# Attention and two expert layers on one core: VectorE's order in the front left to the scheduler, weight conversion cut into pieces, late weight splits spread out

## The chip, the cores and the metric

The kernel runs on one core of a Trainium2 chip. The metric is device time in microseconds for one execution, from the median of several runs. Five engines take part, each with its own in-order queue: TensorE (PE, with its weight loads PEld), VectorE (DVE), ScalarE (ACT), GpSimd (POOL) and SyncE (SP, which here issues nearly all DMAs).

## What is computed

The reference, cut to what matters here:

```python
scores = q @ k.T / 8 + bias; attn = softmax(scores in a causal window of 128)    # 4 x 8 heads, 576 x 64
x = attn @ v                                          # 2304 tokens x 512
h = x @ w_in; g = maximum(0.01 * h, h); x = g @ w_out # d_ff 2048
logits = x @ w_gate                                   # 8 experts
# tokens go to experts by descending logit, at most 288 tokens to an expert
for e in range(8): out[mask_e] = maximum(x[mask_e] @ w1[e], 0) @ w2[e]
```

w_in and w_out arrive as 64-bit floats; the kernel turns them into 32-bit ones on the chip. All large products are made with operands split into a high and a low part (three products each), so every weight needs a copy on ACT (high) and a subtraction on DVE (low).

## The kernel before

There are three stages. The **front** (0 to about 418 us) does attention, the first product (x @ w_in) and the logits; the middle (to about 660 us) does the second product and, beside it, the assignment of tokens; the end runs the eight experts. The change touches the front alone.

The front is a loop over steps s. A step handles one block of 64 queries at several stages of its life: scores of block s+1 on PE, its four score reductions on DVE (L435, `neg` and `nm`) and four exponentials on ACT (L438, `pr`), the weighted sum of block s-1 (L479, `xv`), the transposes of block s (L462, `pt`, copied by ACT as `pts`, L464) and the normalisation of block s+1: DVE makes the reciprocal (L446, L447, `rs`) and ACT multiplies by it (L450; from block 13 on DVE takes half, L452). In every second step ACT copies a finished pair of blocks (L489, `xh`) and DVE subtracts (L490, `xl`). Beside this a step runs up to four **items** before step 16, two from then on: an item is 24 matmuls of x @ w_in into one bank `h` (L504; there are two such banks), ACT's scaled copy `th` (L513) and DVE's maximum into `gb` (L517), which sets the bank free. Items stand in fixed steps: two in 5 and 8, four in 9, 11, 13, 14 and 15, two in each from 17 on.

Sixteen weight tiles are converted, k = 0 to 15, in steps `CONV_AT` = 2, 3, 5, 6, 8, 9, 10, 11, 13, 14, 16, 17, 19, 20, 22, 23. ACT takes the absolute value one step ahead (`conv_abs`, L343). DVE does two operations in `conv_first` (L354, L355) and four in `conv_rest` (L361, L364, L365, L367), all in place on `dt` with a helper `de`. For k < 8 ACT then writes the high part (L348, `wh_in`) as the last thing in the step, and DVE the low part one step later (L371, `wl_in`). For k of 8 and more the result is w_out, written to memory and folded with w_gate on PE (`wtp`, `pg`, `pw`, and `gs` on DVE).

What sets the order: PE, ACT and DVE run in the order in which the program is written (`ENG_A`, `manual_schedule`). So `conv_rest` stands as one block of four behind the first item's `gb`, and `conv_first` behind `xl`. SP and POOL are left to the scheduler.

From step 28 on the loop also loads and splits late tiles (`tail`: three of w_out, two of g, five of w_out) through two staging tiles (L167 `st_out`, L157 `wh_out`, L158 `wl_out`): twice per step it splits the oldest staged tile and stages the next, the first three at once, the others when few items are left. Late logits use bank t, the bank of the transposes; it is set free by a small copy on DVE (L544, `lt`).

Of the kernel before, what the change touches and what calls it, by code (L numbers as in the profile page):

```python
# [33 lines left out]
PTB = 2  # L34
PRB = 2
ET = mybir.EngineType
ENG_A = {ET.PE, ET.Activation, ET.DVE}
F_GE = {32: 6, 64: 9}
F_NB = 3
F_TOT = 6  # L40
# [84 lines left out]
def tile_attn_moe_moe2(ctx: ExitStack, tc: tile.TileContext, q_in, k_in, v, w_in, w_out, w_gate, w1, w2, consts, out):  # L125
    nc = tc.nc
    V, A, T, GP = nc.vector, nc.scalar, nc.tensor, nc.gpsimd
# [28 lines left out]
    def split_weight(st, wh, wl, lo_engine):  # L156
        A.activation(wh, st, AF.Copy)  # L157
        lo_engine.tensor_tensor(out=wl, in0=st, in1=wh.bitcast(F32), op=ALU.subtract)  # L158
# [5 lines left out]
    def stage(src, name, pool=None, after=None):  # L164
        pool = pool or stp
        st = pool.tile([P, 1024], F32, tag="wst", name=f"st_{name}", bufs=2 if pool is stp else 3)
        d = nc.sync.dma_start(st, src)  # L167
        if after is not None:
            tc.add_manual_dep(d.ins, after.ins.name, SYNC, reason="behind the first gather")
        return st  # L170
# [128 lines left out]
    by_hand = ctx.enter_context(ExitStack())  # L299
    by_hand.enter_context(tc.manual_schedule(engines=ENG_A))  # L300
    with ExitStack() as actx:
# [39 lines left out]
        def conv_abs(k):  # L341
            t = cv.tile([P, 1024], F32, tag="dt", name=f"dt_{k}", bufs=DTB)
            A.activation(t, raws[k][:, :, 1].bitcast(F32), AF.Abs)  # L343
            conv[k] = t
# [12 lines left out]
        def conv_rest(k):  # L357

            t = conv[k]
            ti = t.bitcast(I32)  # L360
            V.scalar_tensor_tensor(out=ti, in0=raws[k][:, :, 1], scalar=-0x40000000, in1=ti,  # L361
                                   op0=ALU.bitwise_and, op1=ALU.bitwise_or)
            e = cv.tile([P, 1024], F32, tag="de", name=f"de_{k}", bufs=1)
            V.tensor_single_scalar(e.bitcast(I32), ti, -0x800000, op=ALU.bitwise_and)  # L364
            V.scalar_tensor_tensor(out=e, in0=raws.pop(k)[:, :, 0].bitcast(U32), scalar=2.0 ** -52,  # L365
                                   in1=e, op0=ALU.mult, op1=ALU.mult)
            V.tensor_tensor(out=t, in0=t, in1=e, op=ALU.add)  # L367

        def in_low(k):
            wh, wl = win[k]  # L370
            V.tensor_tensor(out=wl, in0=conv.pop(k), in1=wh.bitcast(F32), op=ALU.subtract)  # L371
# [190 lines left out]
        items = [(c, fp) for c in range(NCH) for fp in range(8)]  # L562
# [19 lines left out]
        if True:  # L582
# [19 lines left out]
            def prepare(j):  # L602

                if j and j % 3 == 0:
                    load_qk(j // 3 + 1)

            ready, in_ready = {}, {}
            s = 0
            pending, low_next = [], []
            tail = [(None, wout, wo_dram[fp], f"out_{fp}") for fp in range(3)]  # L610
# [3 lines left out]
            staged = []  # L614
# [4 lines left out]
            while s <= max(NQ, late_end) or items or pending or tail:  # L619

                now = [x for x in items if max(ready.get(x[0], 1 << 30), in_ready.get(x[1] | 1, 1 << 30)) <= s]
                now = now[:ITEMS_0 if s < ITEMS_S else 2]
                for x in now:
                    items.remove(x)
                k = conv_at.get(s)

                for f in after.pop(s, ()):
                    f[0](*f[1:])
                if s + 1 < NQ:
                    scores(s + 1)  # L630
                    prepare(s + 1)
                for k2 in transposes_of_gate:
                    gate_transpose(k2)
                transposes_of_gate.clear()
                if s + 1 < NQ:
                    softmax_exp(s + 1)
                if 0 < s <= NQ:
                    weighted(s - 1)
                    if (s - 1) % 4 == 3:
                        ready[(s - 1) // 4] = s + XLAG  # L640
                for k2 in products_of_gate:
                    gate_product(k2)
                products_of_gate.clear()
                if s < NQ:
                    transpose_p(s)
                load_v(s + 2)
                if k is not None:
                    conv_first(k)
                if s + 1 < NQ:
                    softmax_norm(s + 1)  # L650
                for k2 in low_next:
                    in_low(k2)
                low_next.clear()
                done, pending = pending, []
                if done and not items and not now:
                    fill(F_A)
                for f in done:
                    f[0](*f[1:])
                for c in loads_late:
                    late_load(c)  # L660
                loads_late.clear()
                if s + 1 in conv_at:
                    conv_abs(conv_at[s + 1])
                for n, (c, fp) in enumerate(now):
                    expand(c, fp, 0)
                    expand(c, fp, 1)
                    expand_out(c, fp)
                    if fp % 2 == 1 and c >= LG0:
                        pending.append((logits, c, fp // 2, gbs[c], "l"))
                        if fp == 7:  # L670
                            at(s + 2, logits_fold, c)
                    if n == 0 and k is not None:
                        conv_rest(k)
                if k is not None:
                    if not now:
                        conv_rest(k)
                    if k < 8:
                        in_high(k)
                        low_next.append(k)
                        in_ready[k] = s + IN_LAG  # L680
                    load_raw(k + RAWB)
                if s == gate_end:
                    cv.release()
                    wpa = ctx.enter_context(tc.tile_pool(name="wpa", bufs=3, side="right"))
                    stp = ctx.enter_context(tc.tile_pool(name="stp", bufs=2, side="right"))
                    late_pool = tc.alloc_tile_pool(name="late", bufs=1, side="right")
                if s == late_end:
                    late_pool.release()
                for _ in range(2):
                    if s > gate_end and tail:  # L690
                        if staged and (len(tail) > 7 or len(items) <= len(tail)):
                            pool, lst, _, name = tail.pop(0)
                            lst.append(weight_tiles(pool or wpa, name))
                            split_weight(staged.pop(0), *lst[-1], V)
                        for _, _, src, name in tail[len(staged):STAGES]:
                            staged.append(stage(src, name))
                s += 1
            fill(F_A2)
            for f in sorted(after):
# [409 lines left out]
```

## Time and profile before

| what | value |
|---|---|
| time, median of 3 runs | 920.09 us (920.0 to 920.4) |
| the profiled execution, its own time | 918.32 us |
| its span, first to last instruction | 916.2 us |
| PE busy | 848.8 us (93%) |
| DVE busy | 526.6 us (57%) |
| ACT busy | 392.8 us (43%) |
| mean granted TensorE clock | 0.96 |

A share of busy time is a mean over stages with different limits. The front has to be read by itself: in its first 180 us PE is busy for four to nine tenths of a slice and its granted clock is below 1, later it is busy nearly all the time. Which engine ends each wait there is read from the waits, the chain that ended last and the timeline.

### The profile page before, as it was taken

The page shows a single profiled execution, that of the slowest core. Times are in us where ns is not written, and L with a number is a line of the kernel's source. Part 1 is how long each engine was busy: PE and PEld are TensorE (multiplying, and loading weights), DVE is VectorE, ACT ScalarE, POOL GpSimd, SP SyncE. Part 2 cuts the span into 40 slices and gives each one's busy share as a digit, 9 for nine tenths or more (in the row PEclk, how much of TensorE's full clock was granted, in tenths as well). Part 3 has the DMA queues.
Part 4 walks back from the last instruction along what each step waited for, and adds up shares of the span by engine and source line. Part 5 has one row for each costly group of instructions (what it writes and reads, how often), then busy time and mean ns, then how long its engine had stood idle before and what let it go on. Part 6 is the DMA issues. An engine that isn't in the chain of part 4 may idle for free.

```text
span 916.2 us, 18584 instructions
## 1 busy us (share of the span) xinstructions
PE 848.8 (93%) x7590; PEld 738.8 (81%) x7590; DVE 526.6 (57%) x1311; ACT 392.8 (43%) x867; POOL 56.0 (6%) x82
## 2 busy tenths in 40 slices
PE   5668878989999899999999999998999999999996
PEld 3557767878889788887677777776889999999995
DVE  3866766376674534247678777676235554555540
ACT  6756453456664544232212121211225555555551
POOL 1000000000000000000000000000020221122211
PEclk9578899989999999999999999998999999999998
DMA  9863644577455996585423324221426655576630
GB/s 292 252 199 107 190 145 136 175 212 218 134 164 145 290 238 171 144 249 145 143 93 107 115 80 131 87 95 55 138 91 190 189 182 170 192 223 203 189 119 26
DMA packets 103636, 147.18 MB, mean 161 GB/s; under 512 B 6144, under 2 KB 74368, under 8 KB 101504
## 3 DMA queue, kind: packets, MB, share of 16 engines
q1 hardware_dynamic: 100480, 136.56, 49.7%
q0 software_dynamic: 3072, 9.44, 3.0%
q8 instruction: 60, 0.98, 0.4%
q14 instruction: 24, 0.20, 0.1%
HBM read 113.21 MB, written 32.77 MB: 159 GB/s over the span
## 4 chain that ended last, share of the span: by engine, by line
PE 68%; DVE 14%; ACT 10%; issue 4%; DMA 1%; POOL 1%; SPq 0%; ACTq 0%; POOLq 0%; DVEq 0%
PE po L221 22%; PE h L504 13%; PE m L987 10%; PE y L1006 10%; ACT pr L438 4%; PE cnt L807 3%; PE lg L531 2%; DVE de L365 2%; DVE gb L517 2%; ACT pr L450 2%; DVE dt L361 2%; PE xv L479 2%; DVE dt L367 2%; PE pt L462 1%; ACT dt L343 1%
## 5 line engine op out<-in xcount | busy, mean ns | idle before, releaser
L221 PE MATMUL po<-wh_out,gol 128*128 128x512 f32 x272 | 112.5, 413 | 4.7 <-DVE gol L189 4.6
L517 DVE TENSOR_TENSOR gb<-h,th 128x512 f32<-128x512 f32 x72 | 49.2, 690 | 112.2 <-ACT th L513 112.2
L504 PE MATMUL h<-xh,wh_in 128*128 128x256 f32 x576 | 98.1, 294 | 14.4 <-DVE gb L517 14.3
L221 PE MATMUL po<-wh_out,goh 128*128 128x512 f32 x272 | 110.9, 408 | 0.0
L221 PE MATMUL po<-wl_out,goh 128*128 128x512 f32 x272 | 110.6, 407 | 0.0
L504 PEld LDWEIGHTS h<-xh,wh_in 128*128 128x128 f32 x576 | 80.5, 197 | 21.8 <-DVE gb L517 16.8
L504 PE MATMUL h<-xh,wl_in 128*128 128x256 f32 x576 | 92.3, 284 | 0.0
L504 PE MATMUL h<-xl,wh_in 128*128 128x256 f32 x576 | 91.3, 282 | 0.0
L181 ACT ACTIVATE goh<-gin 128x1024 fp32r<-128x1024 f32 x34 | 36.0, 1059 | 127.4 <-DMA gin<-g_dram 127.1
L158 DVE TENSOR_TENSOR wl_w<-st_w,wh_w 128x1024 fp32r<-128x1024 f32 x60 | 72.9, 1225 | 24.6 <-ACT wh_w L157 24.1
L513 ACT ACTIVATE th<-h 128x512 f32<-128x512 f32 x72 | 42.0, 593 | 104.0 <-PE h L504 103.9
L504 PEld LDWEIGHTS h<-xh,wl_in 128*128 128x128 f32 x576 | 79.8, 195 | 0.0
L438 ACT ACTIVATE pr<-neg,nm 128x192 f32<-128x192 f32 (+2 forms) x144 | 61.0, 425 | 43.4 <-DVE nm L435 43.2
L504 PEld LDWEIGHTS h<-xl,wh_in 128*128 128x128 f32 x576 | 78.6, 193 | 0.0
L1006 PE MATMUL y<-hh,wh_w 128*128 128x288 f32 x256 | 77.4, 302 | 0.0
L1006 PE MATMUL y<-hh,wl_w 128*128 128x288 f32 x256 | 75.6, 295 | 0.0
L1006 PE MATMUL y<-hl,wh_w 128*128 128x288 f32 x256 | 75.5, 295 | 0.0
L221 PEld LDWEIGHTS po<-wh_out,gol 128*128 128x128 f32 x272 | 51.7, 190 | 16.0 <-DVE gol L189 6.3
L157 ACT ACTIVATE wh_w<-st_w 128x1024 fp32r<-128x1024 f32 x60 | 62.4, 1053 | 0.9 <-DMA st_w<-in_w_dram 0.8
L221 PEld LDWEIGHTS po<-wl_out,goh 128*128 128x128 f32 x272 | 51.7, 190 | 10.3 <-issue 0.2
L221 PEld LDWEIGHTS po<-wh_out,goh 128*128 128x128 f32 x272 | 51.7, 190 | 9.5
L990 DVE SCALAR_TENSOR_TENSOR hl<-m,hh 128x288 fp32r<-128x288 f32 x64 | 29.1, 455 | 51.8 <-ACT hh L989 49.1
(219 smaller groups left out, 1545.6 us busy)
## 6 DMA issues: line engine op xcount, KB each, us to landing
st_w<-in_w_dram SPq DMA_DIRECT2D x64, 512.0 KB, 4.1
g_dram<-gb SPq DMA_DIRECT2D x72, 256.0 KB, 4.3
gin<-g_dram SPq DMA_DIRECT2D x34, 512.0 KB, 3.9
gr<-g_dram SPq DMA_DIRECT2D x48, 256.0 KB, 6.0
v<-in_v_dram SPq DMA_DIRECT2D x28, 384.0 KB, 5.5
raw<-in_w_in_dram SPq DMA_DIRECT2D x8, 1024.0 KB, 7.2
raw<-in_w_out_dram SPq DMA_DIRECT2D x8, 1024.0 KB, 5.5
x_dram<-xo SPq DMA_DIRECT2D x17, 256.0 KB, 2.2
```

What stands on the lines that cost most here:

```text
L157: A.activation(wh, st, AF.Copy)
L158: lo_engine.tensor_tensor(out=wl, in0=st, in1=wh.bitcast(F32), op=ALU.subtract)
L181: A.activation(wh, st, AF.Copy)
L221: T.matmul(po, g, w, start=(k == 0), stop=(k == 47))
L438: A.activation(pr[:, i, :nk], neg[:, a, :nk], AF.Exp, scale=-1.0, bias=nm[:, i:i + 1], accum_out=sm[:, i:i + 1])
L504: T.matmul(hp[:, j, :], w[:, d, j * P:(j + 1) * P], x[:, d, :], start=(k == 0), stop=(k == 11))
L513: A.activation(th, hp, AF.Copy, scale=0.01)
L517: V.tensor_tensor(out=gbs[c][:, o:o + 2, :], in0=hp, in1=th, op=ALU.max)
L807: T.matmul(cnt, ge[:, i, :], oh[:, i, :], start=(i == 0), stop=(i == NB - 1))
L987: T.matmul(hp, w[:, d, :], x[:, d, :], start=(k == 0), stop=(k == 11))
L990: V.scalar_tensor_tensor(out=hl[:, f, :], in0=hp, scalar=0.0, in1=hh[:, f, :].bitcast(F32), op0=ALU.max, op1=ALU.subtract)
L1006: T.matmul(yp, w, x[:, f, :], start=(k == 0), stop=(k == 23))
```

## The change

DVE leaves `ENG_A`: in the front the scheduler now chooses DVE's order, by its own estimate of when each instruction can start; PE and ACT still run as written. `conv_rest` becomes a generator, cut into its four operations, and the step calls it a piece at a time between items (one piece per item with more than two items, two with fewer, the remainder at the end). The first three late tiles are split only when they were staged two or more steps ago, one per step; the other seven keep their rule.

```diff
-ENG_A = {ET.PE, ET.Activation, ET.DVE}
+ENG_A = {ET.PE, ET.Activation}
...
             V.scalar_tensor_tensor(out=ti, in0=raws[k][:, :, 1], scalar=-0x40000000, in1=ti,
                                    op0=ALU.bitwise_and, op1=ALU.bitwise_or)
+            yield
             e = cv.tile([P, 1024], F32, tag="de", name=f"de_{k}", bufs=1)
             V.tensor_single_scalar(e.bitcast(I32), ti, -0x800000, op=ALU.bitwise_and)
+            yield
             V.scalar_tensor_tensor(out=e, in0=raws.pop(k)[:, :, 0].bitcast(U32), scalar=2.0 ** -52,
                                    in1=e, op0=ALU.mult, op1=ALU.mult)
+            yield
             V.tensor_tensor(out=t, in0=t, in1=e, op=ALU.add)
...
+                rest = iter(()) if k is None else conv_rest(k)
                 for n, (c, fp) in enumerate(now):
...
-                    if n == 0 and k is not None:
-                        conv_rest(k)
+                    for _ in range(1 if len(now) > 2 else 2):
+                        next(rest, None)
+                for _ in rest:
+                    pass
                 if k is not None:
-                    if not now:
-                        conv_rest(k)
...
-                for _ in range(2):
+                for _ in range(2 if len(tail) <= 7 else 1):
                     if s > gate_end and tail:
-                        if staged and (len(tail) > 7 or len(items) <= len(tail)):
+
+                        if staged and (staged[0][1] < s - 1 if len(tail) > 7 else len(items) <= len(tail)):
                             pool, lst, _, name = tail.pop(0)
                             lst.append(weight_tiles(pool or wpa, name))
-                            split_weight(staged.pop(0), *lst[-1], V)
+                            split_weight(staged.pop(0)[0], *lst[-1], V)
                         for _, _, src, name in tail[len(staged):STAGES]:
-                            staged.append(stage(src, name))
+                            staged.append((stage(src, name), s))
```

PE's order and POOL's do not move at all, and ACT's only in the three late `wh_out`. The number of instructions is the same but for one DMA. In the changed file lines 364 and on stand one to three lines lower up to L450, and three lower in the rest of the loop (L365, L367, L370 there are L364, L365, L367 here; L449 and L450 are L446 and L447, L520 is L517, L547 is L544).

DVE in step 5 (two items, h_0 and h_1; tile k = 2 is dt_457, tile 3 is dt_527), before:

```order
L446 TENSOR_SCALAR rs_520<-sm_473 128x4
L447 RECIPROCAL rs_520<-rs_520 128x4
L517 TENSOR_TENSOR gb_0_556<-h_0_529,th_0_554 128x512
L361 SCALAR_TENSOR_TENSOR dt_457<-raw_107,dt_457 128x1024
L364 TENSOR_SCALAR de_559<-dt_457 128x1024
L365 SCALAR_TENSOR_TENSOR de_559<-raw_107,de_559 128x1024
L367 TENSOR_TENSOR dt_457<-dt_457,de_559 128x1024
L517 TENSOR_TENSOR gb_0_556<-h_1_563,th_1_588 128x512
```

The same place now:

```order
L361 SCALAR_TENSOR_TENSOR dt_457<-raw_107,dt_457 128x1024
L449 TENSOR_SCALAR rs_520<-sm_473 128x4
L365 TENSOR_SCALAR de_559<-dt_457 128x1024
L450 RECIPROCAL rs_520<-rs_520 128x4
L367 SCALAR_TENSOR_TENSOR de_559<-raw_107,de_559 128x1024
L370 TENSOR_TENSOR dt_457<-dt_457,de_559 128x1024
L354 TENSOR_SCALAR dt_527<-dt_527 128x1024
L520 TENSOR_TENSOR gb_0_556<-h_0_529,th_0_554 128x512
L355 TENSOR_SCALAR dt_527<-dt_527 128x1024
L361 SCALAR_TENSOR_TENSOR dt_527<-raw_314,dt_527 128x1024
L520 TENSOR_TENSOR gb_0_556<-h_1_561,th_1_586 128x512
L365 TENSOR_SCALAR de_668<-dt_527 128x1024
```

Tile 2 is now finished ahead of the first item's maximum, tile 3 is begun a step early between the two maxima, and the reciprocal stands behind two pieces.

DVE in step 9 (four items; tile k = 5 is dt_811, tile 6 is dt_944), before:

```order
L446 TENSOR_SCALAR rs_936<-sm_893 128x4
L447 RECIPROCAL rs_936<-rs_936 128x4
L371 TENSOR_TENSOR wl_in_878<-dt_741,wh_in_877 128x1024
L517 TENSOR_TENSOR gb_0_973<-h_0_946,th_0_971 128x512
L361 SCALAR_TENSOR_TENSOR dt_811<-raw_596,dt_811 128x1024
L364 TENSOR_SCALAR de_976<-dt_811 128x1024
L365 SCALAR_TENSOR_TENSOR de_976<-raw_596,de_976 128x1024
L367 TENSOR_TENSOR dt_811<-dt_811,de_976 128x1024
L517 TENSOR_TENSOR gb_0_973<-h_1_980,th_1_1005 128x512
L517 TENSOR_TENSOR gb_2_1037<-h_2_1010,th_2_1035 128x512
L517 TENSOR_TENSOR gb_2_1037<-h_3_1039,th_3_1064 128x512
```

The same place now:

```order
L449 TENSOR_SCALAR rs_936<-sm_893 128x4
L370 TENSOR_TENSOR dt_811<-dt_811,de_1006 128x1024
L450 RECIPROCAL rs_936<-rs_936 128x4
L354 TENSOR_SCALAR dt_944<-dt_944 128x1024
L520 TENSOR_TENSOR gb_0_973<-h_0_946,th_0_971 128x512
L355 TENSOR_SCALAR dt_944<-dt_944 128x1024
L520 TENSOR_TENSOR gb_0_973<-h_1_976,th_1_1001 128x512
L361 SCALAR_TENSOR_TENSOR dt_944<-raw_675,dt_944 128x1024
L365 TENSOR_SCALAR de_1134<-dt_944 128x1024
L367 SCALAR_TENSOR_TENSOR de_1134<-raw_675,de_1134 128x1024
L520 TENSOR_TENSOR gb_2_1035<-h_2_1008,th_2_1033 128x512
L370 TENSOR_TENSOR dt_944<-dt_944,de_1134 128x1024
```

All six operations on tile 6 have moved out of step 10 in among the maxima of step 9, with one operation at most between the first two maxima.

DVE at the end of step 29, where the late splits stood, before:

```order
L452 TENSOR_SCALAR pr_3841<-pr_3841,rs_3877 128x192 x2
L517 TENSOR_TENSOR gb_0_3911<-h_0_3884,th_0_3909 128x512
L517 TENSOR_TENSOR gb_0_3911<-h_1_3913,th_1_3938 128x512
L158 TENSOR_TENSOR wl_out_3944<-st_out_3800,wh_out_3943 128x1024
L158 TENSOR_TENSOR wl_out_3950<-st_out_3806,wh_out_3949 128x1024
L544 COPY lt<-pl_3955 128x16
L435 ISA neg_0_3972,nm_3969<-s_0_3959,bias_sb 128x192
```

The same place now:

```order
L455 TENSOR_SCALAR pr_3835<-pr_3835,rs_3871 128x192 x2
L520 TENSOR_TENSOR gb_0_3905<-h_0_3878,th_0_3903 128x512
L547 COPY lt<-pl_3937 128x16
L520 TENSOR_TENSOR gb_0_3905<-h_1_3907,th_1_3932 128x512
L438 ISA neg_0_3954,nm_3951<-s_0_3941,bias_sb 128x192
```

Both splits have left the step (the three now stand one each in steps 30 to 32), and the copy that sets bank t free is ahead of the second maximum.

## Rows read from the trace of the kernel before

**Rows 1.** Busy time by stretch: PE, PEld, DVE, ACT, POOL, clock, DMA share, GB/s.

```profile
core 0: us, PE busy (x) PEld busy (x) DVE busy (x) ACT busy (x) POOL busy (x), PEclk, DMA share, GB/s
18.00:166.00 148.00, 111.76 (x1150) 100.71 (x1151) 101.04 (x230) 84.19 (x225) 0.29 (x1) 0.84 0.60 179
166.00:193.00 27.00, 23.62 (x294) 21.48 (x293) 13.00 (x37) 13.72 (x37) 0.00 (x0) 0.89 0.58 164
193.00:312.00 119.00, 117.81 (x1419) 108.73 (x1419) 75.58 (x222) 71.40 (x211) 0.00 (x0) 1.00 0.64 186
312.00:330.00 18.00, 14.90 (x167) 11.98 (x165) 7.64 (x20) 7.91 (x18) 0.00 (x0) 0.81 0.96 243
```

**Rows 2.** Waits: who waited for whom, total us, times, longest us.

```profile
ACT wh_in L348 <- DVE dt L367: 18.8, 6, 4.2
...
ACT pr L450 <- DVE rs L447: 15.4, 12, 1.9
...
PE h L504 <- DVE gb L517: 14.3, 11, 3.3
```

**Rows 3.** Chain that ended last, steps 5 and 6: start, us, what.

```profile
43.00 1.02 ACT dt L343
...
49.14 0.49 ACT th L513
49.65 0.69 DVE gb L517
50.34 1.14 DVE dt L361
51.51 0.71 DVE de L364
52.24 1.24 DVE de L365
53.50 1.24 DVE dt L367
54.76 1.06 ACT wh_in L348
...
58.08 0.69 DVE xl L490
58.77 0.61 DVE dt L354
...
60.39 1.11 DVE wl_in L371
...
65.92 1.06 ACT wh_in L348
```

**Rows 4.** The same chain: a reduction, and the exponentials that begin step 12.

```profile
128.02 0.26 DVE neg L435
128.32 1.86 ACT pr L438 x8
```

**Rows 5.** Timeline of steps 10 and 11: idle time before and its releaser in brackets.

```profile
105.23 1.50 ACT L450 ACTIVATE pr<-pr,rs 128x192 f32<-128x192 f32 x4 [1.90 <-DVE rs L447]
...
110.66 1.06 ACT L348 ACTIVATE wh_in<-dt 128x1024 fp32r<-128x1024 f32 x1 [2.90 <-DVE dt L367]
...
117.07 0.74 PE L504 MATMUL h<-xh,wh_in 128*128 128x256 f32 x4 [3.30 <-DVE gb L517]
```

**Rows 6.** Timeline of PE in step 16.

```profile
186.16 0.63 PE L402 MATMUL pw<-cst,gs 128*128 128x32 f32 x4 [2.64 <-DVE gs L395]
```

**Rows 7.** Timeline of PE in step 30.

```profile
318.18 1.06 PE L462 MATMUL pt<-cst,pr 128*96 128x128 f32 x4 [3.10 <-DVE lt L544]
```

**Rows 8.** The chain: two items in steps 30 and 31.

```profile
320.25 7.37 PE h L504 x48
...
332.95 5.67 PE h L504 x48
```

## The prediction, made before the changed kernel ran

> **What bounds the kernel now.** I read the busy time by stretch first [rows 1], then the waits [rows 2], then the chain that ended last [rows 3, 4]. The stretches show three regimes in the front. From 18 to 166 us (steps 2 to 14) no engine is full: PE 111.8 of 148 us at a granted clock of 0.84, DVE 101.0, ACT 84.2. From 193 to 312 us (steps 17 to 29) PE is busy for 117.8 of 119 us at clock 1.00, so it is the bound, and DVE and ACT have a third to spare. From 312 to 330 us PE is held up again, at clock 0.81.
>
> Why nobody is full early shows in the waits: ACT waits 18.8 us, in six waits, for a converted tile before it can write the high part, 15.4 us for reciprocals, and PE 14.3 us in eleven waits for a maximum that would free its bank [rows 2]. The chain shows how these hang together in step 5 [rows 3]: the first item's `th` at 49.14, its maximum at 49.65, and only then L361, L364, L365, L367 one behind another until 54.73, then `wh_in` at 54.76. DVE runs the four pieces behind a maximum that has to wait for PE and ACT, though their tile was ready at 44.02 (the end of L343). ACT cannot go on, since `wh_in` stands ahead of the next step's exponentials in its queue. So it is a ring: ACT waits for the conversion, the conversion for an item, the item for PE, PE for the last step's ACT. PE's and ACT's orders stay, so only DVE's part of this ring can become shorter. Every step keeps its items; a step that ends earlier lets all later ones start earlier, up to the middle stage, where PE is again the bound.
>
> **The change, part by part.** I walk the new DVE order with the durations of the chain. *Steps 5 and 6.* The absolute value ends at 44.02. L354 takes 0.61, and L355 I count as L364, 0.71; then L361 1.14, reciprocal and sum 0.3, L364 0.71, L365 1.24, L367 1.24: tile 2 is done near 50.0 instead of 54.73. `wh_in` now waits for the second item's `th`, which ends near 52.2, so it begins about 2.5 us sooner. What is late next is the exponentials: DVE has put L354, L355 and L361 of tile 3 and the two maxima (0.69 each) ahead of the reductions, so they start only near 54.9, 0.9 sooner than at the end of `wh_in` before (55.82). But tile 3 is then three parts done. After the low part (1.11), four reductions (0.26 each [rows 4]), `xl` 0.69, L365 and L367 it ends near 61.1; the reciprocal follows, ACT normalises, and `wh_in` starts near 62.8 instead of 65.92: 3.1 us for the two steps.
>
> *The other steps by the same walk.* Steps 2 to 4: the conversions no longer wait behind `xl` and the reductions are done while ACT still writes `wh_in`: 1.4 us. Steps 8 and 9: about 1.9 gained in step 8 as in step 5, 0.9 lost in step 9, where the reciprocal is put behind a low part and two pieces, so that the absolute value and the first `th` come later: 1.0 us. Step 10 has no item, and its tile was converted in step 9 while DVE waited for `th`: ACT's two waits there, 1.90 and 2.90 [rows 5], go: 4.8 us. Step 11: the four pieces leave the gap between the first two maxima, so the 3.30 us that PE waited [rows 5] go; the reciprocal behind two pieces costs 0.9: 2.4 us. I thus put the exponentials that began at 128.32 [rows 4] near 115.6, a sum of 12.7.
>
> Steps 13 and 14: of the 14.3 us that PE waits for maxima I count 4.4 there; tile 8's L367 and tile 9's L354 now stand ahead of step 13's first maximum and make PE wait some 2.4: 2.0 us. Step 16 has no item, and PE is idle for 3.4 of the 27 us around it [rows 1]: `gs` stood behind `xl` and made PE wait 2.64 us [rows 6]; now it is the first thing after the reductions: 2.5 us. Steps 17 to 28: PE is full [rows 1], so I take nothing. One piece between maxima is covered by 5.67 us of item work per step [rows 8]; without that cover each would cost its 0.7 to 1.2 us.
>
> *Late splits.* In step 29 two splits stand ahead of `lt`, the copy that frees the transposes' bank, and the second waited for its load. PE waits 3.10 us [rows 7], and the two items behind it take 7.37 us instead of 5.67 at the lower clock [rows 1, 8]: 3.1 + 1.7 = 4.8 us. Now the loads are two steps old and one split per step (1.1 us on DVE, as L371 in rows 3) lies beside 5.67 us of items.
>
> *What it adds.* The reductions now run bank by bank, so ACT's second exponential waits for the third reduction: 3 x 0.26 = 0.78 us after the start, against 0.26 + 1.86/4 = 0.73 when ACT gets to it. An estimate of 0.1 us a step; where a piece stands between them too, 0.7. The walk has it. On SP the loads of raw tiles are ahead of some loads of v and stores of g. A raw load waits for L365 of the tile three before, which now comes sooner, and DMA is busy for 0.60 of the stretch [rows 1]: nothing, at most the few us below.
>
> The sum: 1.4 + 3.1 + 1.0 + 4.8 + 2.4 + 2.0 + 2.5 + 4.8 = 22.0 us. The span of 916.2 becomes 894.2. The profiled execution took 918.32, 2.1 more than its span, and the median 920.09, 1.8 more than that; I add both: 898.1, forecast **898 us**.
>
> **The rivals.** *Larger.* PE ran at 0.84 of its clock in the early stretch [rows 1], a mixture of 1.2 and 2.4 GHz, while it kept waiting; with fewer gaps it may stay at the upper level. The walk keeps PE's old durations. A mean of 0.84 between 0.5 and 1 is 0.32 of 148 us at the lower level, 47 us; at PE's mean busy share of 0.76 that is 36 us of work, which takes 18 at full speed. If half of the 18 us lies on the ring, up to 9 more are gained: 889. The Trainium skill ("TensorE: Matmul & The Clock Gate", part 1 on the clock gate) says that the throttled state is the default and activity releases it; by that rule the gain is on this side, and the trace agrees in so far as 0.84 and 0.81 stand where PE waits and 1.00 where it is full.
>
> *Smaller.* The scheduler placed DVE's instructions by estimates, and loads may keep their old pace: DMA share 0.60 is a mean, with full slices among it. If half of steps 2 to 14's 14.7 us is lost, the time is 898 + 7.4 = 905; if nearly all is, 912.
>
> *Slower, by the reciprocals.* In the new order pieces stand ahead of the reciprocal: in step 3 L361, L364 and four reductions (2.9), in 5 L361 and L364 (1.85), in 6 L365, `xl`, four reductions and L367 (4.2), in 9 L364, a low part, L365 and L367 (4.3), in 11 as in 5 (1.85): 15.1 us. ACT's normalisation waits for them, and everything behind it in ACT's queue: the absolute values, `th`, and through it PE. If that, not the conversion's end, ends these steps, nothing is gained in steps 2 to 14 and 15.1 are lost: 920.1 + 15.1 - 2.5 - 4.8 = 928. It decides once ACT reaches the normalisation before the pieces are done by more than `wh_in` waited. For it speak 15.4 us of waits for reciprocals now, against it that the larger waits are those for the tiles, and that the pieces moved ahead are the tile that ACT waits for next.
>
> *The front's gain doesn't arrive.* If PE were the hidden bound early too, only the late 4.8 would come: 915. Its 36 us idle before 166 us speak against it.
>
> **How the numbers follow.** The forecast (890 to 904) has 0.60. The larger gain, 880 to 890, 0.13. Smaller gains and only the late part, 904 to 917, 0.18. Within 0.2% (918.2 to 921.9) 0.03; 0.2% is about what a measurement of this kernel tells from no change. Slower, about 928, 0.06. So faster 0.91. The range from 885 to 912 leaves out about 0.06 below, 0.05 of the smaller gains, and the 0.09 of the last two cases.
>
> **What would show it.** In the profile after: ACT's waits for tiles fall from 18.8 us to a few, PE's for maxima from 14.3 to under 6, the waits for reciprocals stay or grow; the exponentials of step 12 start near 115.6; no wait of 3 us in step 30; items of steps 17 to 28 still end to end. If the reciprocal waits grow by more than the tile waits fall, the walk is wrong in the reciprocal's place; if the exponentials of step 12 come early and the front still ends near 418, PE had a bound that I do not see; if SP's loads end PE's or ACT's waits, it was the queue.

## The result, and the profile after

| | before | after |
|---|---|---|
| time, median | 920.05 us (917.8 to 920.4, 4 runs) | 892.19 us (891.14 to 894.0, 4 runs) |
| ratio | | 0.9704, 95% interval 0.9682 to 0.9727 |
| profiled execution; its span | 918.32; 916.2 us | 894.0; 892.2 us |
| mean granted TensorE clock | 0.960 | 0.972 |

The change saves 27.9 us in the medians and 24.0 us between the two profiled spans. The changed file has three more lines ahead of most places, so L504 of before is L507 after, L435 is L438, L450 is L453 and so on; in `conv_rest` L364, L365 and L367 are now L365, L367 and L370.

Busy time by stretch in the profile after, columns as in [rows 1]; the four stretches end within 3 us of the same points of the work as those of before:

```profile
18.00:150.00 132.00, 105.92 (x1144) 95.90 (x1142) 97.97 (x228) 84.88 (x224) 0.93 (x1) 0.87 0.68 203
150.00:176.00 26.00, 23.55 (x305) 21.42 (x302) 17.11 (x50) 15.88 (x45) 0.00 (x0) 0.93 0.71 205
176.00:294.00 118.00, 117.87 (x1419) 109.56 (x1419) 70.29 (x213) 69.23 (x201) 0.00 (x0) 0.99 0.61 175
294.00:309.00 15.00, 15.00 (x217) 12.23 (x215) 7.52 (x27) 8.41 (x24) 0.00 (x0) 1.00 0.94 245
```

Against [rows 1], the first stretch is 16 us shorter (15.3 us between the first exponentials of steps 2 and 15; the rest is its end, which lies that much earlier in the work), and DVE does about the same work in it (97.97 us against 101.04). PE's work between those two points takes 5.1 us less (105.79 against 110.92) at a higher clock (0.87 against 0.84); the rest of the gain is idle time. The third stretch, where PE is full, hardly changes: 118 us against 119. The fourth is 3 us shorter and PE has no gap left in it.

Waits of the front in the profile after (engine, line waited for, us in total, times, longest):

```profile
ACT pr L453 <- DVE rs L450: 14.3, 12, 2.7
...
PE xv L482 <- ACT pr L453: 10.4, 3, 5.9
...
PE h L507 <- DVE gb L520: 4.1, 2, 3.8
...
ACT wh_in L348 <- DVE dt L370: 1.7, 2, 0.9
...
DVE xl L493 <- ACT xh L492: 0.7, 1, 0.7
```

Against [rows 2], ACT's wait for a converted tile went from 18.8 to 1.7 us, and PE's for maxima from 14.3 to 4.1. ACT's wait for reciprocals stayed (14.3 against 15.4). DVE's own wait at `xl` for ACT's copy `xh`, which was 33.9 us in 18 in the profile before (the experiments come back to it), is 0.7.

The line on PE's 10.4 us at `xv` has to be read with care. It names a normalisation, but `xv` reads only `pts` and `v`. The place at 41.84, `xl` on DVE and then `xv` on PE:

```profile
41.08 0.66 DVE L493 TENSOR_TENSOR xl<-xv,xh 128x512 fp32r<-128x512 f32 x1
```

```profile
41.84 1.25 PE L482 MATMUL xv<-pts,v 96*64 96x64 f32 x32 [2.19 <-ACT pr L453]
```

The products of a new pair go into the one bank of `xv` (`bufs=1`), which `xl` still reads; they start 0.10 us after `xl` ends, here and at 100.32 (2.29 us). So two of the three waits are for `xl`. The third, 5.93 us at 34.48, ends as a load of `v` lands (34.35); in a second execution of the same kernel (`after_again` below) the profile gives that wait to the load itself:

```profile
33.27 1.97 PE L482 MATMUL xv<-pts,v 96*64 96x64 f32 x32 [4.27 <-DMA v<-in_v_dram]
```

None of this is new in kind: in the profile before `xv` also starts 0.10 us after `xl` ends, at 41.23, 58.87, 103.62 and 131.49, under the name of `pts`.

The chain that ended last, steps 5 and 6, after (start, us, what), against [rows 3]:

```profile
43.82 0.70 DVE dt L354
...
50.68 0.07 DVE gb L520
...
51.91 1.22 DVE dt L361
...
53.14 0.60 DVE gb L520
53.74 0.60 DVE de L365
54.34 0.26 DVE neg L438
...
57.64 0.16 DVE rs L449
...
58.06 0.60 DVE xl L493
...
59.50 1.14 DVE dt L370
60.63 0.10 DVE rs L450
...
62.31 0.16 ACT wh_in L348
```

The first item's maximum at 50.68 is no longer followed by four pieces: those of tile 2 are over, and what stands there (L361, L365) is tile 3, a step early. `xl` at 58.06 has no idle time in front of it. The second `wh_in` starts at 62.31 instead of 65.92.

Start of a step's first exponential on ACT, from the timelines. The differences are as read; the first loads of this execution came 0.57 us later, and no row takes that off:

| step | before | after | gained |
|---|---|---|---|
| 2 | 19.30 | 19.88 | -0.57 |
| 5 | 43.93 | 43.69 | 0.24 |
| 7 | 66.88 | 63.16 | 3.72 |
| 9 | 85.00 | 78.52 | 6.48 |
| 10 | 100.45 | 96.22 | 4.23 |
| 12 | 128.32 | 116.91 | 11.41 |
| 16 | 182.72 | 168.01 | 14.71 |
| 17 | 192.86 | 173.00 | 19.86 |
| 18 | 202.68 | 185.68 | 17.00 |
| 28 | 296.67 | 278.87 | 17.80 |
| 31 | 330.73 | 307.43 | 23.30 |

### The profile page after: what moved, and what is told of

Its sections match the earlier page's. It is cut to its first block, busy times and chain, and to the rows that moved or that the text cites. A ratio compares the mean times of both kernels' runs of the same rounds, so it can differ in the third digit from the quotient of the medians.

```text
span 892.2 us, 18599 instructions
## 1 busy us (share of the span) xinstructions
PE 839.7 (94%) x7590; PEld 732.4 (82%) x7590; DVE 523.0 (59%) x1311; ACT 394.1 (44%) x867; POOL 56.4 (6%) x82
## 4 chain that ended last, share of the span: by engine, by line
PE 81%; DVE 8%; ACT 5%; issue 4%; POOL 1%; DMA 0%; SPq 0%; POOLq 0%; ACTq 0%; DVEq 0%
PE po L221 23%; PE h L507 21%; PE m L992 11%; PE y L1011 10%; PE xv L482 3%; PE pt L465 3%; PE cnt L812 3%; PE lg L534 2%; PE s L423 2%; ACT pr L453 2%; ACT pr L441 2%; DVE dt L361 1%; PE wtp L386 1%; PE yo L1021 1%; ACT dt L343 1%
## 5 line engine op out<-in xcount | busy, mean ns | idle before, releaser
L507 PE MATMUL h<-xh,wh_in 128*128 128x256 f32 x576 | 96.7, 292 | 4.1 <-DVE gb L520 4.1
L520 DVE TENSOR_TENSOR gb<-h,th 128x512 f32<-128x512 f32 x72 | 49.7, 690 | 80.6 <-ACT th L516 77.1
L507 PE MATMUL h<-xh,wl_in 128*128 128x256 f32 x576 | 91.2, 281 | 0.0
L507 PE MATMUL h<-xl,wh_in 128*128 128x256 f32 x576 | 90.6, 280 | 0.0
L507 PEld LDWEIGHTS h<-xh,wh_in 128*128 128x128 f32 x576 | 80.3, 196 | 9.1 <-DVE gb L520 4.5
L507 PEld LDWEIGHTS h<-xh,wl_in 128*128 128x128 f32 x576 | 78.9, 193 | 0.0
L507 PEld LDWEIGHTS h<-xl,wh_in 128*128 128x128 f32 x576 | 77.7, 190 | 0.0
```

Of the source, the lines that this page charges most:

```text
L507: T.matmul(hp[:, j, :], w[:, d, j * P:(j + 1) * P], x[:, d, :], start=(k == 0), stop=(k == 11))
L520: V.tensor_tensor(out=gbs[c][:, o:o + 2, :], in0=hp, in1=th, op=ALU.max)
```

## The experiments

The theory on record was the ring of the prediction: ACT waits for the conversion, the conversion for an item, and the new order cuts the conversion's part. The rivals were that the late rule carries the gain, that cutting into pieces does, or that another wait of DVE is what counts. The kernel before ran beside each group at 918.3 to 920.1 us.

### The two halves apart

`late_only` is the kernel before with the late rule alone.

> The kernel before with the late-split rule of the change alone (a tile is split only two steps after it was staged, one per step); VectorE stays in hand order. Theory: the stall of step 30 (3.10 us of waiting for the small copy, and 1.7 us of items at the lower clock) is a cost of its own: about 915 us against 920, no PE wait of 3 us between the transposes of step 30. Rival (the stall only moves, since the splits still have to be done in steps in which PE is full): about 920.

Measured: 912.39 us, ratio 0.9934 (0.9916 to 0.9952). No step before 29 starts earlier by more than 0.5 us; step 30 starts 4.4 and step 31 5.6 us earlier. So alone the late rule is worth 6 us, as the theory had it (it expected 5).

`front_only` is the changed kernel with the late rule of before.

> The changed kernel with the late-split rule of before; VectorE's order in the front is the scheduler's, with the pieces. Theory (the parts add up): 892 plus the 5.3 us that the late steps gained in the changed kernel, 897; the exponentials of step 12 start near 117 us as in the changed kernel. Rival (the scheduler puts the small copy that frees the transposes' bank ahead of the two splits, so the stall goes without the new rule): 893, and no PE wait on that copy in step 30.

Measured: 890.36 us, ratio 0.9698 (0.9663 to 0.9734), no slower than the whole change. The rival holds: beside the scheduler's order the late rule adds nothing. DVE's timeline of step 30 (start, us, engine and line, operation, operands, idle time before and its releaser) shows why, first of before, then of `front_only`:

```profile
316.72 1.23 DVE L158 TENSOR_TENSOR wl_out<-st_out,wh_out 128x1024 fp32r<-128x1024 f32 x1 [1.61 <-ACT wh_out L157]
317.86 0.17 DVE L544 COPY lt<-pl 128x16 f32<-128x16 f32 x1
```

```profile
290.50 0.17 DVE L547 COPY lt<-pl 128x16 f32<-128x16 f32 x1 [1.74 <-PE pl L545]
290.78 0.69 DVE L520 TENSOR_TENSOR gb<-h,th 128x512 f32<-128x512 f32 x1
...
294.65 1.23 DVE L158 TENSOR_TENSOR wl_out<-st_out,wh_out 128x1024 fp32r<-128x1024 f32 x1 [0.94 <-ACT wh_out L157]
```

The split still waits for its staged tile, but now `lt` stands ahead of it and PE waits for nothing. The two halves repair the same 3 us wait [rows 7], so 27.9 and 6 us do not add.

### The pieces without the scheduler

`pieces_by_hand` is the changed kernel with DVE in the written order: pieces between the items of their own step, and the new late rule.

```diff
-ENG_A = {ET.PE, ET.Activation}
+ENG_A = {ET.PE, ET.Activation, ET.DVE}
```

> The changed kernel with VectorE put back into the hand order: the pieces stand where the loop calls them, one behind each maximum in steps of four items, two in steps of two, and the late rule is the new one. Theory (what pays is that a tile is begun before the item's maximum, a step early): most of the front's gain is missing; PE's waits for maxima fall from 14.3 to about 6 us, the waits of ACT for tiles stay near 15 us; about 909 us. Rival (what pays is that the maxima are no longer behind four pieces): about 895 us.

Measured: 911.31 us, ratio 0.9927 (0.9900 to 0.9954), 1.1 us below `late_only`. PE's waits for maxima fall to 7.4 us in three, but ACT's for tiles grow to 24.3 in eight. So the rival fell. The theory's time held, but not its waits: the one for tiles was to stay near 15. The cutting alone is worth about 1 us, which is within the spread of the runs (909.5 to 912.1 against 910.8 to 914.5). Under the scheduler it is worth nothing: with the conversion written as one block of four again, the scheduler's order is the same on every engine, row for row.

### Is the conversion on the ring?

Both kernels without L364, L365 and L367 (the helper, and the product and sum that add the low word of the 64-bit weight); in the kernel before:

```diff
-            e = cv.tile([P, 1024], F32, tag="de", name=f"de_{k}", bufs=1)
-            V.tensor_single_scalar(e.bitcast(I32), ti, -0x800000, op=ALU.bitwise_and)
-            V.scalar_tensor_tensor(out=e, in0=raws.pop(k)[:, :, 0].bitcast(U32), scalar=2.0 ** -52,
-                                   in1=e, op0=ALU.mult, op1=ALU.mult)
-            V.tensor_tensor(out=t, in0=t, in1=e, op=ALU.add)
+            raws.pop(k)
```

> The kernel before with the last three operations on each of the sixteen tiles left out (L364, L365, L367: the low word is not added). Theory (the conversion is part of the ring that sets the early steps): 3.1 us in each of the eight steps up to step 11, and the waits behind them: 890 to 900 us. Rival (the conversion only lies beside waits for items): 912 us or more.

> The changed kernel with the same three operations left out. Theory (in the new order the conversion has mostly left the path, but still stands ahead of reciprocals in steps 3, 6 and 9): 883 to 889 us, so a loss of less than half of what the kernel before loses. Rival (it is as much on the path as before): 870 us or less.

Measured: 889.3 us (just under the theory's range), 29.7 below before, step 12 starting 21.2 us earlier; and 879.64 us, 12.6 below the changed kernel. So the conversion was on the ring, as the theory says, and the new order hides more than half of what it cost. The second result is lower than expected and lies between the two ranges: even now part of the conversion is on the path.

### A step early, by hand

`early_by_hand`: the changed kernel with DVE in the written order (and so with the new late rule), all six operations of a tile in one generator that begins between the items of the step before; the remainder stands behind the reciprocal and the low part.

```diff
-ENG_A = {ET.PE, ET.Activation}
+ENG_A = {ET.PE, ET.Activation, ET.DVE}
...
-                if k is not None:
-                    conv_first(k)
...
                 low_next.clear()
+                for _ in rest:
+                    pass
...
                     conv_abs(conv_at[s + 1])
-                rest = iter(()) if k is None else conv_rest(k)
+                    rest = conv_all(conv_at[s + 1])
```

This copies the most visible trait of the scheduler's order, L361 of tile 3 between the maxima of step 5.

> VectorE in hand order, with the tiles begun early by hand: all six operations on a tile are called a piece at a time behind the maxima of the step before its own, the remainder after the next step's reciprocal and low part; the reciprocals stand ahead of all pieces, the reductions run as before, the late rule is the new one. Theory (what paid was that a tile is begun a step early, while VectorE waits for items; the scheduler is only the means): 890 to 896 us, against 911 for the pieces by hand in the tile's own step. Rival (it needs the free order, piece by piece): 903 to 910 us.

Measured: 909.19 us, ratio 0.9904 (0.9878 to 0.9929). **The theory fell**, and the time lies in the rival's range: beyond the late rule the early pieces bring 3 us. The waits of steps 2 to 15 in its profile:

```profile
DVE xl L490 <- ACT xh L489: 15.3, 7, 3.6
...
PE h L504 <- DVE gb L517: 14.4, 4, 5.4
ACT wh_in L348 <- DVE dt L367: 12.1, 6, 5.1
DVE rs L446 <- ACT pr L438: 11.5, 7, 2.2
```

DVE itself waits 26.8 us at `xl` and at the reciprocal, and the ready pieces are behind it in its queue. That gave a new theory: what pays is that ready pieces stand ahead of the instructions that wait for ACT.

### Moving only xl

The wait at `xl` in the whole front of the kernel before, which the prediction had not used:

```profile
DVE xl L490 <- ACT xh L489: 33.9, 18, 3.7
```

`xl_late` is the kernel before with one subtraction moved: `xl` is written behind the reciprocal and the low part instead of right behind the reductions.

```diff
-                V.tensor_tensor(out=xl, in0=x, in1=xh.bitcast(F32), op=ALU.subtract)
+                xl_next.append((xl, x, xh))
...
                     in_low(k2)
                 low_next.clear()
+                for xl, x, xh in xl_next:
+                    V.tensor_tensor(out=xl, in0=x, in1=xh.bitcast(F32), op=ALU.subtract)
+                xl_next.clear()
```

> The kernel before with one edit: VectorE's subtraction xl, which waits for ScalarE's copy xh in 18 steps (33.9 us of idle VectorE in all, 1.9 us each in the trace of before), is written behind the reciprocal and the low part instead of right behind the row maxima. Theory (what VectorE loses is time at the head of its queue, with ready tile pieces behind an instruction that waits for ScalarE): xl's wait nearly goes, about eight of the 18 lie in steps with a tile, and half of their 1.9 us each and more reaches the ring: 906 to 913 us. Rival (a wait that is taken away at xl comes back at the reciprocal, which waits for the exponentials right behind it; early_by_hand lost its time there): the wait of rs for pr grows by about what xl's falls, and the time stays at 916 to 919.

Measured: 906.71 us, ratio 0.9869 (0.9852 to 0.9886). The theory's range holds. DVE's timeline of step 6, before and then `xl_late`:

```profile
56.07 0.35 DVE L435 CUSTOM_DVE_ANT_0 neg<-s,bias_sb 128x192 f32<-128x192 f32 x1
...
58.08 0.69 DVE L490 TENSOR_TENSOR xl<-xv,xh 128x512 fp32r<-128x512 f32 x1 [1.65 <-ACT xh L489]
58.69 0.69 DVE L354 TENSOR_SCALAR dt<-dt 128x1024 f32<-128x1024 f32 x1
```

```profile
54.12 0.35 DVE L435 CUSTOM_DVE_ANT_0 neg<-s,bias_sb 128x192 f32<-128x192 f32 x1
...
54.40 0.69 DVE L354 TENSOR_SCALAR dt<-dt 128x1024 f32<-128x1024 f32 x1
55.12 0.69 DVE L355 TENSOR_SCALAR dt<-dt 128x1024 int32<-128x1024 int32 x1
55.73 0.16 DVE L446 TENSOR_SCALAR rs<-sm 128x4 f32<-128x4 f32 x1
...
57.14 0.68 DVE L655 TENSOR_TENSOR xl<-xv,xh 128x512 fp32r<-128x512 f32 x1
```

PE's next products in the kernel before:

```profile
58.87 1.97 PE L479 MATMUL xv<-pts,v 96*64 96x64 f32 x32 [1.43 <-ACT pts L464]
```

Before, DVE stands idle for 1.65 us at `xl` although tile 3 is ready for L354. With `xl` moved, L354 starts right behind the reductions, and by the time `xl` comes its input has long been there. A place further back has its price, since `xv` waits for `xl` (58.08 + 0.69 = 58.77, then 58.87 in the kernel before): measured from the reductions, `xl` and with it `xv` come 1.0 us later. Up to step 16 the move gains 7.3 us. Steps 16 to 22 give 7 more, of which 5.2 are PE's busy time in the same steps (67.50 us before, 62.33 here) at a clock of 1.00 instead of 0.95. Whether the move caused that higher clock is not settled (see the last section); the profiled execution took 903.02 us, the shortest of four and 3.7 below the median.

### The two edits by hand

`fill_by_hand` is `early_by_hand` with `xl` moved like this and with three of the tile's pieces between the reductions and the reciprocal (the remainder moves too, to right behind the reciprocal, ahead of the low part); `early_xl_late` has the move of `xl` alone.

```diff
+FILL = 3
...
+                for _ in range(FILL):
+                    next(rest, None)
                 if s + 1 < NQ:
                     softmax_norm(s + 1)
+                for _ in rest:
+                    pass
```

> VectorE's order by hand again, the late rule of the change, and two edits against early_by_hand: three of the tile's six pieces (those not yet done behind the items' maxima of the step before) stand between the row maxima and the reciprocal, the rest behind the reciprocal, and xl stands behind the low part. Theory (the gain comes from ready pieces that stand ahead of instructions that wait for ScalarE, the reciprocal and xl): 892 to 900 us, most of the scheduler's gain, VectorE's waits of rs for pr and of xl for xh under 8 us together against 60 in early_by_hand, ScalarE's waits for tiles under 8. Rival (no fixed place in the step does it, the scheduler's own choice per step is needed, and the reciprocal now comes late): 903 to 910 us, with ScalarE's or TensorE's waits behind the normalisation grown.

> early_by_hand (909.2 us) with one edit: xl stands behind the reciprocal and the low part; the tile's pieces stay where early_by_hand has them, behind the reciprocal, and no piece is put between the row maxima and the reciprocal. It parts fill_by_hand (893.4 us, 16 us below early_by_hand), which has both edits. Theory (the place of xl is what early_by_hand lacked; before with xl moved gave 12.8 us, so the same here): 895 to 899 us, and the three pieces ahead of the reciprocal bring the remaining 2 to 5. Rival (the two edits are needed together, since pieces behind the reciprocal still stand behind a wait): 901 to 907 us, with ScalarE's waits for tiles above 8 us.

Measured: `fill_by_hand` 893.35 us, ratio 0.9727 (0.9711 to 0.9744), the changed kernel's time within the intervals, with an order written by hand. `early_xl_late` 904.73 us, 0.9840 (0.9823 to 0.9857): here the rival's range was right: the move alone gives 4.5 us, the pieces on top of it 11.4. The pieces without the move were not run, so it is not shown that they need it. DVE's timeline of step 6 in `fill_by_hand`:

```profile
51.90 1.22 DVE L365 SCALAR_TENSOR_TENSOR de<-raw,de 128x1024 f32<-128x1024 uint32 x1
53.15 1.22 DVE L368 TENSOR_TENSOR dt<-dt,de 128x1024 f32<-128x1024 f32 x1
54.29 0.16 DVE L447 TENSOR_SCALAR rs<-sm 128x4 f32<-128x4 f32 x1
...
55.69 0.69 DVE L659 TENSOR_TENSOR xl<-xv,xh 128x512 fp32r<-128x512 f32 x1
```

Two ready pieces fill the 2.4 us between the reductions and the reciprocal, while ACT makes the exponentials, and neither the reciprocal nor `xl` waits. In `early_xl_late` the wait that was taken from `xl` comes back at the reciprocal:

```profile
DVE rs L446 <- ACT pr L438: 22.4, 14, 3.2
...
ACT wh_in L348 <- DVE dt L367: 9.0, 5, 3.7
```

For each kernel, from the waits between 18 us and step 16's first exponential, and what it gains on before at that exponential:

| kernel | DVE waits at rs + xl, us | ACT waits for tiles, us | gained by step 16 | time, us |
|---|---|---|---|---|
| before | 4.8 + 15.4 | 18.8 | | 920.1 |
| early_by_hand | 11.5 + 15.3 | 12.1 | -0.7 | 909.2 |
| xl_late | 8.0 + 0 | 18.0 | 7.3 | 906.7 |
| early_xl_late | 22.4 + 0 | 9.0 | 5.3 | 904.7 |
| fill_by_hand | 5.5 + 0 | 1.6 | 18.2 | 893.4 |
| after | 3.3 + 0 | 1.7 | 14.7 | 892.2 |

(`xl_late` alone lacks the late rule's 6 us.) Only where DVE's waits and ACT's waits for tiles are both small is the gain large. The gains are those of one profiled execution each: that of `xl_late` was 3.7 us below its median and that of `fill_by_hand` 3.0, that of after 1.8 above; the second execution of after gains 16.2 by step 16. So the order of the last two rows in that column means nothing. One expectation missed: in the whole front of `fill_by_hand` DVE still waits 25.9 us at the reciprocal, not under 8. Of these, 20 lie behind step 16, where few pieces are left to fill with and PE is the bound.

### The reciprocal that comes late

`rs_one` is the changed kernel without the addition of 1e-9 ahead of the reciprocal; `front_rs_one` has the late rule of before as well.

```diff
-            V.tensor_scalar(rs, sm, 1e-9, None, op0=ALU.add)
-            V.reciprocal(rs, rs)
+            V.reciprocal(rs, sm)
```

> The changed kernel without the addition of 1e-9 ahead of the reciprocal (a sum of exponentials with the largest at 1 is at least 1, so the addition changes nothing in 32 bits); the reciprocal is then one instruction, and the scheduler puts it where the addition stood, ahead of the pieces that stood between. Theory (the late reciprocal gives back part of the gain: 2.2 us in step 9, 0.6 us in step 4, some in steps 3, 5 and 6): 886 to 889 us, ACT's waits for reciprocals from 14.3 to under 9 us. Rival (the pieces that stood ahead are what ends the step in any case): 891 to 892 us, with larger waits of ACT for converted tiles.

> The changed kernel with the late rule of before (front_only, 890.4 us) and the reciprocal as one instruction, without the addition of 1e-9 ahead of it (rs_one, 889.1 us). Theory (the gain of the shorter reciprocal, 2 to 3 us, lies in steps 2 to 14, that of the old late rule, if any, in steps 28 to 31, so they add): 886.5 to 889 us. Rival (front_only's 1.8 us against the changed kernel is the step-17 clock fall that only some executions have, and rs_one's is in part the same): 889 to 891 us.

Measured: `rs_one` 889.09 us, ratio 0.9682 (0.9646 to 0.9717); ACT's waits for reciprocals fall from 14.3 to 1.7 us:

```profile
ACT pr L452 <- DVE rs L449: 1.7, 4, 0.8
```

The scheduler had parted the two instructions by a piece or by reductions (L449 at 57.64 and L450 at 60.63 in the chain of after), and with one instruction there is nothing to part. But other waits are longer in this profile: those for tiles from 1.7 to 5.0 us, and PE's for maxima from 4.1 to 9.1. Step 9, where 2.2 us were expected, is no shorter: 17.74 us against 17.70 in the changed kernel, though ACT's wait for the reciprocal there fell from 2.69 to 0.77. `front_rs_one` took 889.37 us, 0.9685 (0.9670 to 0.9700), 1 us below `front_only`: the rival's range. These two are the fastest full kernels, some 3 us below the changed one, and their intervals overlap with its own.

### The changed kernel once more

> The changed kernel once more, to set it beside the others on one chip. Step 29 to 31 and the stretch after step 16 are read again: its first profile showed TensorE at 0.57 of its clock from 172 to 180 us, and the kernel with the old late rule, with the same instructions there and the same two waits of 1.65 and 0.80 us, showed 1.00. Theory (the clock's fall there comes by chance): the runs spread over some 3 us, 889 to 893. Rival (the new late rule costs 1.8 us): 892 in every run.

Measured: 892.19 us, ratio 0.9711 (0.9695 to 0.9728), the same median. The four runs, 890.61 to 892.68, lie in the theory's range, but three of them at 892, as the rival had it. So it stays open whether the new late rule costs `front_only`'s 1.8 us; set against the kernel before that ran beside each, the two ratios overlap. Its profiled span is 888.7 us instead of 892.2; step 16 starts at 166.48 and step 18 at 181.33, where the first execution had 168.01 and 185.68. So two executions of one kernel differ by 3.5 us in their spans, and most of it has a place, told in the last section.

## Why the prediction was right, point by point

The forecast was 898 us (885 to 912), the measurement 892.19: the sign and the steps in which the gain lies were as in the likeliest case, the cause was right in part only, and the gain was 6 us larger than the sum. Its terms against the starts of the steps:

| term | predicted, us | measured in the profile after, us |
|---|---|---|
| steps 2 to 4 | 1.4 | 0.8 |
| steps 5 and 6 | 3.1 | 3.5 |
| steps 8 and 9 | 1.0 (1.9 - 0.9) | 0.5 (2.75 - 2.25) |
| step 10 | 4.8 | 4.9 |
| step 11 | 2.4 | 2.3 |
| steps 12 to 14 | 2.0 | 3.3 |
| step 16 and the start of 17 | 2.5 | 5.15, then -2.86 lost in step 17 |
| steps 17 to 28, the rest | 0 | 0.8 |
| late splits | 4.8 | 5.5 |

- **Step 12's exponentials** were put near 115.6 and began at 116.91, with 0.57 us of that from the later first loads. The walk by durations of the chain was good to 1 us over twelve steps; in the second execution they began at 115.57.
- **What the walk had wrong in kind.** The prediction explained the ring by the pieces standing behind an item's maximum. Pieces freed from that place alone gave 1 us. What the runs showed in its place is that DVE waits at the head of its queue, at `xl` and the reciprocal, with a ready tile behind. The walk got the sizes right since it followed the new order, in which this is mended as well, but the text names `xl` only for steps 2 to 4 and 16, and has no word of PE's wait for it at `xv`. DVE's wait at `xl` is not among [rows 2], though at 33.9 us in 18 (15.4 of it up to step 16) it was larger than any of them.
- **Step 16** was the most undersized term: 2.5 us counted for `gs`; 5.15 came. ACT's wait of 3.09 us at step 17's first exponential (192.86), for reductions that stood behind tile 10's four pieces, went as well and was not counted. In that execution 2.86 were lost again to the clock (in `after_again` 5.15 came as well, and 0.04 went).
- **Larger** (889, the clock) was true of the clock, and little of the time: PE's busy time from step 2 to step 15 fell by 5.1 us, where the sum held it fixed, but the steps up to step 15 gained 15.3 us (without the later first loads) against 14.7 in the sum. By the Trainium skill ("TensorE: Matmul & The Clock Gate", part 1 on the clock gate), activity releases the throttle; this stretch agrees, with 0.87 where PE waits less against 0.84. In step 17, in the last section, PE's instructions and waits are the same and the clocks are not.
- **Slower, by the reciprocals** had the wrong sign, and the mechanism is small: ACT's waits for reciprocals did not grow as a whole, PE's 10.4 us at `xv` are not waits for a normalisation (see the profile after), and taking the delay away (`rs_one`) gave 1 to 3 us, not 15. Step 9 loses 2.25 us where 0.9 were counted for the late reciprocal, but with the reciprocal early (`rs_one`) it is as long; what costs it is not shown. PE waits there 3.79 us for one maximum, 4.71 in `rs_one`.
- **Late splits** came to about the predicted size, but not through the new rule: `front_only` has them without it. The sum counted a gain of the rule which the scheduler's order brings anyway; the two are not separate parts of a sum.
- **The front's gain doesn't arrive** (915) fell: steps 17 to 28 stay end to end (117.87 of 118 us busy), and start 16 to 22 us earlier.

Of the 6 us between forecast and measurement, 2.0 are the terms above (a span of 892.2 instead of 894.2). The other 3.9 are what the forecast added to the span for the way from there to the median: before's profiled execution was faster than its median, after's slower, and after's median, 892.19, equals its profiled span by chance. In the second execution (span 888.7) the terms alone give 27.5 us, and step 17 loses nothing; the closeness of the sum of spans, 22.0 against 24.0, is in part luck.

## What to carry to other kernels

Look in the waits for an engine that waits often and briefly at its own queue's head, even if no one seems to wait for it, and ask what ready work stands behind that instruction: moving one subtraction that waits 1.9 us in 18 steps gained 13 us here, and filling the wait before a reciprocal with ready pieces 11 us (904.7 to 893.4). Try such edits together: in `early_xl_late` the wait taken away at `xl` came back at the reciprocal, the next instruction that needs the same engine (11.5 us there became 22.4). And ask which engine waits for the instruction that is moved back: here PE's `xv` waits for `xl`. Before crediting parts of a change, run them apart in both directions: the late rule was worth 6 us alone and nothing beside the other part.

## What the runs showed of the hardware

The granted clock of a stretch is not fixed by the program. In step 17 PE runs the same instructions after the same two waits (1.65 us at `xv`, which ends with `xl`, and 0.80 for `wg`) in both executions of the changed kernel and in `front_only`. Busy time, columns as in [rows 1], from 3.99 to 11.99 us after step 16's first exponential, in the changed kernel's first execution, then in its second:

```profile
172.00:180.00 8.00, 7.20 (x59) 6.57 (x55) 6.43 (x11) 4.11 (x14) 0.00 (x0) 0.57 0.75 182
```

```profile
170.47:178.47 8.00, 7.20 (x84) 6.86 (x80) 6.88 (x12) 4.71 (x15) 0.00 (x0) 1.00 0.76 195
```

One execution ran that stretch mostly at the lower of the two levels (1.2 GHz) and the other at the upper (2.4 GHz): in the same 7.20 us of busy time 59 and 84 matmuls. `front_only` had 1.00 too. The first one's two items took 7.34 us instead of 5.72, and step 18 came 2.9 us later against before than step 17 did. What made the clock fall there is not shown. The same chance may be a part of why `xl_late` gains in steps 16 to 22, where its clock is 1.00 and before's is 0.95: with one profile of each it stays open how much of that the moved instruction caused.

DVE hands a bank on to PE in about 0.10 us: between 18 and 180 us PE began `xv` 0.09 to 0.11 us after the end of `xl` in five places in each of the two profiles of the changed kernel. The waits there bear ACT's names (`pts` or `pr`) all the same. So compare the end of a wait with the ends of all instructions that share its operands or its bank, on every engine, before believing the name beside it.
